# A fused retention and MLP kernel: chunk 0 of q and v loaded by SyncE as float32, a second bank for the first transposes, and four split units of the first product

## The chip, the cores and the metric

The kernel runs on one core of one Trainium2 chip. The metric is the time of one execution on the device in microseconds (us), lower is better; a kernel's time is the median of its runs. The five engines are PE (TensorE), DVE (VectorE), ACT (ScalarE), POOL (GpSimd) and SP (SyncE). Each takes its own instructions strictly in the order written, and they meet at semaphores.

## The reference

```python
def _attn_ref(q, k, v):                       # each (8, 8, 576, 64) float32
    scores = np.matmul(q, k.transpose(0, 1, 3, 2)) / np.sqrt(D_)
    gamma = 1.0 - 2.0 ** (-5.0 - np.arange(H))
    rel = pos[:, None] - pos[None, :]
    Dmat = np.where(rel >= 0, gamma[:, None, None] ** rel[None, :, :], 0.0)
    return np.matmul(scores * Dmat[None], v)
...
x = attn_out.transpose(0, 2, 1, 3).reshape(B * S, H * D)      # (4608, 512)
h = x @ w_in                                                  # (512, 2048)
g = h * (1.0 / (1.0 + np.exp(-1.702 * h)))
out = g @ w_out                                               # (2048, 512)
```

Attention without a softmax: each score is multiplied by gamma(head) to the power of the distance, and by zero for later keys. The two matrix products after it are most of the arithmetic.

## The kernel before, in words

**Recording.** The kernel is written as a list. `R.op(engine, function, reads, writes, banks)` (class `Rec`, line 43) appends one operation to its engine's queue and works out its waits from the named tiles and PSUM banks. So the order in which the Python calls stand is the order in which each engine works; there is no planner. An engine whose next operation waits does nothing else meanwhile.

**Attention of batch 0** works in chunks of 128 tokens: chunks 0 to 3 first, chunk 4 (64 tokens) later. For a chunk `n`:

- `load(0, n, "qkv")` (line 206) has POOL issue one DMA each for q, k and v, which turns float32 in DRAM into bfloat16 in `st_q`, `st_k`, `st_v`.
- `transposes(n)` (369) turns q and k on PE into the PSUM bank W (`psT`); `evac_t(n)` (378) copies the bank to `qk` on ACT.
- `intra(n)` (498) is `scores(n)` on PE into bank S, then `mask_s(n)` on DVE, which multiplies the scores by the mask into `sm`. For chunk 3 the mask is `mask3`, which has the decay factor in it, and `values(3)` takes v unscaled for the scores' part and the scaled copy `v3` for the state.
- `scale_v(n)` (352) multiplies v by the decay `vfac`: chunk 0 on DVE, chunks 1, 2 and 3 on POOL.
- `values(n)` (405) is three groups of eight matmuls on PE: scores times v, the running state k times v in bank Z, and q times the state so far (`zq`). With `z_last` the state comes last.
- `evac_z(n)` (465) copies the state on ACT; `evac_o(n)` (475) multiplies the result by `gq` on DVE and writes x transposed, `xT`, for the chunk's 128 tokens.

`later_gq` and `constants_first` make the decay tables with Exp on ACT; `fill(count)` (804) are matmuls of zeros that only keep PE running.

**The first product** of the 512 tokens of chunks 0 to 3 consists of 16 units f = 0 to 15 (`hidden`, 689): four matmuls of 512 columns with the weights `w_in`, then Gelu on ACT into `gT`. Unit f needs the weights' piece f // 2. The weights come in pieces `load_w_in(lo, hi)` (236): (0,1) for f = 0, 1; (1,2) for f = 2, 3; (2,4) for f = 4 to 7; (4,6); (6,8). Units 0 and 1 are made by `hidden_split` (704): first the columns of chunks 0 to 2 (0:384), then the columns of chunk 3 (384:512). The second product with `w_out` (`project`, 743) and the attention of batches 1 to 7 (`burst`) follow, unit by unit, with PE as the bound.

**The order around the change** is lines 786 to 876. POOL's queue: two iotas, the loads q0, k0, q1, k1, q2, k2, v0, q3, k3, v1, v2, v3, the weights (0,1), (1,2), (2,4), three `scale_v`, the other weights. PE's: 14 fills, turn 0, 4 fills, scores 0, turn 1, 3 fills, scores 1, turn 2, 3 fills, scores 2, turn 3, values 0, 3 fills, scores 3, values 1, 2 and 3, units 0 to 15. DVE's, after the constants: mask 0, mask 1, scale v0, mask 2, out 0, mask 3, out 1, out 2, out 3 ("mask n" is `mask_s(n)`, "out n" is `evac_o(n)`); then until about 35 us the memsets `constants_third`, `constants_shifted` and the swaps of `regroup`.

Of the kernel before, what the change touches and what calls it, by code (L numbers as in the profile page):

```python
# [131 lines left out]
def bass_retnet_parallel__then__act_gelu_quick_kernel(  # L132
# [11 lines left out]
    with es:  # L144
        def sb(name, shape, dtype):
            return es.enter_context(nc.sbuf_tensor(name, shape, dtype))
# [11 lines left out]
        tiny = sb("tiny", [P, 1], FP32)  # L158
        idle = sb("idle", [P, 512], BF16)
        lng = sb("lng", [P, HP], FP32)  # L160
        vraw = sb("vraw", [P, H, NC], FP32)
        vfac = [sb(f"vfac{i}", [P, H, NC], FP32) for i in range(2)]
        zacc = sb("zacc", [P, 3, 2 * 128], FP32)
# [30 lines left out]
        def gamma(h):  # L194
            return 1.0 - 2.0 ** (-5.0 - h)
# [40 lines left out]
        def load_w_in(lo, hi):  # L236

            cols = slice(256 * lo, 256 * hi)
            s = moe_w_in.rearrange("(a p) n -> p a n", p=128)[:, :, cols]
            R.op("POOL", lambda e: e.dma_start(w_in_sb[:, :, cols], s),  # L240
                 w=[("w_in", i) for i in range(lo, hi)], dma=("w_in", lo))
# [7 lines left out]
        def iota(t, name, pattern, base, mul):  # L249
            R.op("POOL", lambda e: e.iota(t.ap(), pattern, base=base, channel_multiplier=mul,  # L250
                                          allow_small_or_imprecise_dtypes=True), w=[name])

        def constants_first():
            iota(posj, "posj", [[128, NC]], 0, 1)
            iota(posa, "posa", [[1, 128]], 0, 0)
            R.op("DVE", lambda e: e.tensor_scalar(
                rel.ap(), posa.ap(), posj[:, 0:1], None, ALU.subtract),
                r=["posa", "posj"], w=["rel"])
            R.op("DVE", lambda e: e.memset(idle.ap(), 0.0), w=["idle"])
            for hp in range(HP):  # L260
                for hh in range(2):
                    R.op("DVE", lambda e, hp=hp, hh=hh: e.memset(
                        lng[64 * hh : 64 * hh + 64, hp : hp + 1],
                        math.log(gamma(2 * hp + hh))), w=[("lng", hp, hh)])
            R.op("DVE", lambda e: e.tensor_single_scalar(ident.ap(), rel.ap(), 0.0, ALU.is_equal),
                 r=["rel"], w=["ident"])
            R.op("DVE", lambda e: e.tensor_single_scalar(mask.ap(), rel.ap(), 0.0, ALU.is_ge),
                 r=["rel"], w=["mask"])
            for c in range(1, NC):
                R.op("DVE", lambda e, c=c: e.tensor_single_scalar(  # L270
                    posi[:, c - 1, :], posa.ap(), 128.0 * c, ALU.add), r=["posa"], w=["posi"])
            for h in range(H):
                R.op("ACT", lambda e, h=h: e.activation(
                    vraw[:, h, :], posj.ap(), AF.Exp, scale=-math.log(gamma(h))),
                    r=["posj"], w=["vraw"])
            for hp in range(HP):
                R.op("ACT", lambda e, hp=hp: e.activation(
                    gq[:, hp, 0:128], posa.ap(), AF.Exp, scale=lng[:, hp : hp + 1]),
                    r=["posa", ("lng", hp, 0), ("lng", hp, 1)], w=[("gq", 0)])
            R.op("DVE", lambda e: e.tensor_single_scalar(  # L280
                vfac[0].ap(), vraw.ap(), float(QK_SCALE), ALU.mult), r=["vraw"], w=[("vfac", 0)])

        def constants_second():
            R.op("DVE", lambda e: e.memset(zs.ap(), 0.0), w=[("zs", 0), ("zs", 1)])
# [67 lines left out]
        def scale_v(n, eng="DVE", to=None):  # L352
            b, c = divmod(n, NC)
            sl = b % NST
            t = st_v[:, sl, c, :].rearrange("p (h d) -> p h d", d=DH)
            f = vfac[min(b, 1)][:, :, c : c + 1].to_broadcast([P, H, DH])
            if to is None:
                R.op(eng, lambda e: e.tensor_tensor(t, t, f, ALU.mult),  # L358
                     r=[("vfac", min(b, 1))], w=[("v", sl, c)])
                return  # L360
            o = to.rearrange("p (h d) -> p h d", d=DH)
            R.op(eng, lambda e: e.tensor_tensor(o, t, f, ALU.mult),
                 r=[("vfac", min(b, 1)), ("v", sl, c)], w=[v3_key])

        def sides(n):
            b, c = divmod(n, NC)
            return [(0, st_q, "q", b % NST, c), (1, st_k, "k", b % NST, c)]

        def transposes(n):
            def fn(e):  # L370
                for a, t, nm, sl, c in sides(n):
                    for hp in range(HP):
                        i = e.matmul(psT[:, a, hp, :], t[:, sl, c, 128 * hp : 128 * hp + 128],  # L373
                                     ident.ap(), is_transpose=True)
                return i
            R.op("PE", fn, r=["ident"] + [(nm, sl, c) for a, t, nm, sl, c in sides(n)], ps=["W"])

        def evac_t(n):
            R.op("ACT", lambda e: e.activation(qk[n % NQK].ap(), psT, AF.Copy),  # L379
                 w=[("qk", n % NQK, 0), ("qk", n % NQK, 1)], ps=["W"])  # L380

        def half(r):
            return slice(64 * r, 64 * r + 64)
# [114 lines left out]
        def intra(n):  # L498
            scores(n)
            mask_s(n)  # L500
# [183 lines left out]
                R.op("DVE", lambda e: e.tensor_copy(z, zacc[:, 0 : len(gs), :]), r=r, w=["zw"])  # L684


        hbanks = [(psH[0], ("H", 0)), (psH[1], ("H", 1)), (psU, "U")]

        def hidden(c, f, at, ahead=()):
            bank, key = at  # L690
            toks = range(8 * c, 8 * c + 8)
# [1 line left out]
            def fn(e):  # L693
                for a in range(4):
# [9 lines left out]
        def hidden_split(fs):  # L704

            for lo, hi in ((0, 384), (384, 512)):
                for f in fs:
                    bank, key = hbanks[2 * f]

                    def fn(e, f=f, bank=bank, lo=lo, hi=hi):  # L710
                        for a in range(4):
                            i = e.matmul(bank[:, lo:hi], w_in_sb[:, a, 128 * f : 128 * f + 128],
                                         xT[:, a, lo:hi], start=(a == 0), stop=(a == 3))
                        return i
                    R.op("PE", fn, r=[("w_in", f // 2)]
                         + [("xT", x) for x in range(lo // 64, hi // 64)], ps=[key])
            for f in fs:
                bank, key = hbanks[2 * f]
                R.op("ACT", lambda e, f=f, bank=bank: e.activation(  # L719
                    gT[0][:, f, :], bank.ap(), AF.Gelu_apprx_sigmoid), w=[("gT", 0, f)], ps=[key])  # L720

        def hidden_half(c, half, f, at, ahead=()):
            bank, key = at
# [80 lines left out]
        def fill(count):  # L804
            def fn(e):
                for _ in range(count):
                    i = e.matmul(psH[0].ap(), idle[:, 0:128], idle.ap(), start=True, stop=True)
                return i
            R.op("PE", fn, r=["idle"], ps=[("H", 0)])
# [5 lines left out]
        fill(14)  # L815
# [36 lines left out]
        constants_third(0, NST)  # L852
        constants_shifted()
# [11 lines left out]
        turns = [0]  # L865
# [171 lines left out]
```

## Time and profile before

| | |
|---|---|
| median of 3 runs (lowest, highest) | 301.7 us (301.42, 302.22) |
| the profiled execution's own time | 302.22 us |
| its span, from first to last instruction | 300.4 us |
| busy share of the span: PE, DVE, ACT, POOL | 97%, 41%, 43%, 52% |
| granted TensorE clock | 0.999 |

The profiled execution is the slowest of the three; 1.8 us of its time lie outside the span. Times on the timeline are microseconds from the span's start. A line of the timeline gives the start, the duration, engine, source line, operation, the tile written and the tiles read, the shapes and the count, and in brackets how long the engine was idle before and who released it. Durations of consecutive operations on one engine overlap a little: the multiply by the mask lasts 1.23 us, but the next operation starts 1.14 us after it, and the 0.68 us of an `evac_o` are 0.60 to 0.62 us from start to start.

### The profile page before, as it was taken

How to read it: one execution, taken by the hardware profiler on the slowest of the kernel's cores; microseconds unless marked ns; L12 is line 12 of the kernel's file. 1: busy time of each engine (PE TensorE's matmuls, PEld its weight loads, DVE VectorE, ACT ScalarE, POOL GpSimd, SP SyncE). 2: the span in 40 equal slices, each digit the busy share in tenths (PEclk: the TensorE clock that was granted, in tenths of full speed). 3: DMA queues.
4: the chain of work that ended last, by engine and by line, in shares of the span. 5: the costliest groups of instructions: out<-in, count | busy, mean ns of one | idle time of the engine just before them, and what ended most of it. 6: DMA issues, size and time to landing. Idle time of an engine off the chain costs nothing.

```text
span 300.4 us, 7696 instructions
## 1 busy us (share of the span) xinstructions
PE 292.5 (97%) x3395; PEld 148.9 (50%) x3395; DVE 122.3 (41%) x213; ACT 127.9 (43%) x215; POOL 154.8 (52%) x208
## 2 busy tenths in 40 slices
PE   7899999899999999999999999999999999999996
PEld 3454455757645444444444444544444444444444
DVE  6589735362525555334506143265236503000012
ACT  7676426614445503560375036602570266026600
POOL 8999679998967868677985796000000000000000
PEclk9999999999999999999999999999999999999999
DMA  9999999999999999999999999904720210020012
GB/s 69 145 183 207 177 171 161 193 129 138 178 143 163 163 117 191 173 136 142 135 213 138 127 186 155 85 1 101 173 41 2 105 37 2 0 107 35 0 57 85
DMA packets 154850, 35.78 MB, mean 119 GB/s; under 512 B 145472, under 2 KB 150336, under 8 KB 154816
## 3 DMA queue, kind: packets, MB, share of 16 engines
q0 software_dynamic: 118384, 18.36, 95.8%
q1 hardware_dynamic: 36432, 16.92, 31.6%
q8 instruction: 27, 0.44, 0.6%
q14 instruction: 7, 0.06, 0.1%
HBM read 36.70 MB, written 9.44 MB: 154 GB/s over the span
## 4 chain that ended last, share of the span: by engine, by line
PE 88%; POOL 4%; DMA 3%; ACT 2%; DVE 1%; issue 1%; POOLq 0%
PE psH L746 27%; PE psH L695 24%; PE psU L746 13%; PE psU L695 12%; DMA w_in_sb<-in_moe_w_in_dram 3%; PE psA L560 2%; PE psA L588 2%; PE psH L730 2%; PE psA L602 1%; PE psA L576 1%; POOL st_q L216 1%; PE psA L746 1%; POOL st_k L216 1%; PE psA L772 1%; POOL st_v L216 1%; ACT qk L379 1%
## 5 line engine op out<-in xcount | busy, mean ns | idle before, releaser
L746 PE MATMUL psH<-w_out_sb,gT 128*128 128x512 bf16 x368 | 87.0, 379 | 0.0
L695 PE MATMUL psH<-xT,w_in_sb 128*128 128x512 bf16 x332 | 79.2, 379 | 0.2 <-DMA w_in_sb<-in_moe_w_in_dram 0.2
L649 DVE TENSOR_TENSOR xT<-psA,gq 128x768 bf16<-128x768 f32 x21 | 20.1, 958 | 115.2 <-PE psA L576 115.2
L700 ACT ACTIVATE gT<-psH 128x512 bf16<-128x512 f32 x83 | 49.5, 597 | 26.0 <-PE psH L695 26.0
L229 POOL DMA_DIRECT2D st_k<-in_k_dram x70 | 53.0, 782 | 14.1 <-DMA st_k<-in_k_dram 13.1
L746 PEld LDWEIGHTS psH<-w_out_sb,gT 128*128 128x128 bf16 x368 | 35.0, 98 | 40.7 <-DVE sm L660 0.4
L229 POOL DMA_DIRECT2D st_v<-in_v_dram x70 | 52.0, 770 | 6.0 <-DMA st_v<-in_v_dram 4.0
L695 PEld LDWEIGHTS psH<-xT,w_in_sb 128*128 128x128 bf16 x332 | 32.1, 98 | 38.6 <-DMA w_in_sb<-in_moe_w_in_dram 0.7
L695 PE MATMUL psU<-xT,w_in_sb 128*128 128x512 bf16 x172 | 44.2, 379 | 0.1
L746 PE MATMUL psU<-w_out_sb,gT 128*128 128x512 bf16 x176 | 43.9, 379 | 0.0
L216 POOL DMA_DIRECT2D st_q<-in_q_dram x40 | 36.0, 899 | 9.7 <-DMA st_q<-in_q_dram 7.3
L755 ACT ACTIVATE osb<-psH 128x512 f32<-128x512 f32 x21 | 12.5, 597 | 57.6 <-PE psH L746 54.5
L700 ACT ACTIVATE gT<-psU 128x512 bf16<-128x512 f32 x43 | 25.7, 597 | 13.5 <-PE psU L695 13.5
L695 PEld LDWEIGHTS psU<-xT,w_in_sb 128*128 128x128 bf16 x172 | 16.5, 98 | 20.0 <-ACT gT L719 0.6
L746 PEld LDWEIGHTS psU<-w_out_sb,gT 128*128 128x128 bf16 x176 | 16.6, 98 | 19.4 <-issue 0.5
L358 DVE TENSOR_TENSOR st_v<-st_v,vfac 128x512 bf16<-128x512 bf16 x37 | 24.2, 683 | 0.9 <-DMA st_v<-in_v_dram 0.9
L676 DVE TENSOR_TENSOR zacc<-zacc,psA 128x256 f32<-128x256 f32 x49 | 20.5, 418 | 8.3 <-PE psA L588 7.1
L755 ACT ACTIVATE osb<-psU 128x512 f32<-128x512 f32 x10 | 6.0, 597 | 33.0 <-PE psU L746 33.0
L660 DVE TENSOR_TENSOR sm<-psA,maskw 128x768 bf16<-128x768 f32 x21 | 19.9, 948 | 0.0
L379 ACT ACTIVATE qk<-psA 128x1024 bf16<-128x1024 bf16 x10 | 10.2, 1022 | 10.5 <-PE psA L373 10.5
L758 DVE COPY osb<-psH 128x512 f32<-128x512 f32 x2 | 1.4, 692 | 26.9 <-PE psH L746 26.9
L560 PEld LDWEIGHTS psA<-sm,st_v 64*64 64x64 bf16 x504 | 7.5, 108 | 9.4 <-issue 8.7
(103 smaller groups left out, 231.0 us busy)
## 6 DMA issues: line engine op xcount, KB each, us to landing
out_dram<-osb SPq DMA_DIRECT2D x35, 256.0 KB, 4.0
st_q<-in_q_dram POOLq DMA_DIRECT2D x32, 128.0 KB, 7.2
st_k<-in_k_dram POOLq DMA_DIRECT2D x57, 64.0 KB, 7.5
st_v<-in_v_dram POOLq DMA_DIRECT2D x57, 64.0 KB, 7.3
w_out_sb<-in_moe_w_out_dram POOLq DMA_DIRECT2D x4, 512.0 KB, 11.8
w_in_sb<-in_moe_w_in_dram POOLq DMA_DIRECT2D x3, 512.0 KB, 8.9
st_k<-in_k_dram POOLq DMA_DIRECT2D x4, 128.0 KB, 4.5
st_v<-in_v_dram POOLq DMA_DIRECT2D x4, 128.0 KB, 4.6
```

The costliest lines, as they stand in the source:

```text
L216: paced(R.op("POOL", lambda e, d=d, s=s: e.dma_start(d, s), w=[(nm, sl, c)], dma=(nm, sl, c), own=pace()))
L229: paced(R.op("POOL", lambda e: [e.dma_start(d, s) for d, s in parts], w=[(nm, sl, c)], dma=(nm, sl, c), parts=2, own=pace()))
L358: R.op(eng, lambda e: e.tensor_tensor(t, t, f, ALU.mult), r=[("vfac", min(b, 1))], w=[("v", sl, c)])
L379: R.op("ACT", lambda e: e.activation(qk[n % NQK].ap(), psT, AF.Copy), w=[("qk", n % NQK, 0), ("qk", n % NQK, 1)], ps=["W"])
L560: i = e.matmul(psA[half(t), 2 + u, at : at + 64], rows_of(st_v, m_out, g, u, 4 * u + 2 * t + j), smw[si(m_out)][half(r), j, 2 * blk + t, : ...
L649: R.op("DVE", lambda e: e.tensor_tensor(xT[:, :, t0 : t0 + 192].rearrange("p (u j) n -> p u j n", u=2), psA[:, 2:4, 0:384].rearrange("p u ...
L660: R.op("DVE", lambda e: e.tensor_tensor(o, i, k, ALU.mult), r=["maskw"], w=[("sm", si(m))], ps=["S"])
L676: R.op("DVE", lambda e, to=to, src=src, was=was: e.tensor_tensor(to, was, src, ALU.add), r=[("zacc", (blk - 1) % 3)], w=[("zacc", blk)], p ...
L695: i = e.matmul(bank, w_in_sb[:, a, 128 * f : 128 * f + 128], xT[:, a, 512 * c : 512 * c + 512], start=(a == 0), stop=(a == 3))
L700: R.op("ACT", lambda e: e.activation(gT[c % 2][:, f, :], bank, AF.Gelu_apprx_sigmoid), w=[("gT", c % 2, f)], ps=[key])
L746: i = e.matmul(bank, gT[c % 2][:, f, 128 * r : 128 * r + 128], w_out_sb[:, f, :], start=(f == 0), stop=(f == NF - 1))
L755: R.op("ACT", lambda e: e.activation(osb[m].ap(), bank, AF.Copy), w=[("osb", m)], ps=[key])
```

## The change

- **Loads.** q and v of chunk 0 are no longer loaded by POOL with a cast. SP issues them as float32 into two pieces of `gT[1]` that are unused then (`early(0)`, `early(1)`). DVE casts q0 into `st_q`; `scale_v(0)` reads the float32 v0 and writes `st_v`, and stands right after the constants instead of after turn 2.
- **POOL's queue** becomes: k0, two iotas, q1, k1, v1, q2, k2, v2, q3, `scale_v(1)`, k3, w_in (0,1) and (1,2), v3, w_in (2,4), `scale_v(3)`, w_in (4,6) and (6,8), w_out. `scale_v(2)` moves from POOL to DVE, between out 1 and out 2.
- **Banks.** The transposes of chunks 1 and 3 go to bank H0 (`psH[0]`) instead of W; the fills go to H1.
- **Constants.** The zeros for the fills and the logarithms come before anything that waits for POOL; eight Exp become one; `mask` and three of four `posi` come after `scale_v(0)`.
- **PE's order:** 13 fills, turn 0, 3 fills, turn 1, scores 0, 2 fills, turn 2, scores 1, values 0, 2 fills, scores 2, values 1, 3 fills, turn 3, values 2, scores 3, units 0 and 1 on columns 0:384, values 3, units 2 and 3 on columns 0:384, units 0 to 3 on columns 384:512, then units 4 to 15 whole. Unit 4 goes to bank S.
- **DVE's order** from mask 0 on: mask 0, mask 1, out 0, mask 2, out 1, scale v2, out 2, the memset `zs`, mask 3, out 3.

```diff
+        def load_early(i, src):
+            s = src[0, :, 0:128, :].rearrange("h p d -> p h d")
+            d = early(i).rearrange("p (h d) -> p h d", d=DH)
+            R.op("SP", lambda e: e.dma_start(d, s), w=early_keys(i), dma=("early", i))
...
+            R.op("ACT", lambda e: e.activation(vraw.ap(), vraw.ap(), AF.Exp, scale=-1.0), w=["vraw"])
...
+            R.op("DVE", lambda e: e.tensor_copy(st_q[:, 0, 0, :], early(0)),
+                 r=early_keys(0), w=[("q", 0, 0)])
             R.op("DVE", lambda e: e.tensor_single_scalar(
                 vfac[0].ap(), vraw.ap(), float(QK_SCALE), ALU.mult), r=["vraw"], w=[("vfac", 0)])
+            scale_v(0)
+            for c in range(2, NC):
+                position(c)
+            R.op("DVE", lambda e: e.tensor_single_scalar(mask.ap(), rel.ap(), 0.0, ALU.is_ge),
+                 r=["rel"], w=["mask"])
...
+            if n == 0:
+                i = early(1).rearrange("p (h d) -> p h d", d=DH)
+                R.op(eng, lambda e: e.tensor_tensor(t, i, f, ALU.mult),
+                     r=[("vfac", 0)] + early_keys(1), w=[("v", sl, c)])
+                return
...
+        def turned(n):
+            if n < NC - 1 and n % 2:
+                return psH[0].ap().bitcast(BF16).rearrange("p (a h n) -> p a h n", a=2, h=HP), ("H", 0)
+            return psT, "W"
...
+        constants_zero()
+        load_early(0, q)
+        load_early(1, v)
+        load(0, 0, "k")
         constants_first()
-        for c in range(3):
-            load(0, c, "qk")
-        load(0, 0, "v")
-        load(0, 3, "qk")
-        for c in range(1, 4):
-            load(0, c, "v")
+        load(0, 1, "qk")
+        load(0, 1, "v")
+        load(0, 2, "qk")
+        load(0, 2, "v")
+        load(0, 3, "q")
+        scale_v(1, "POOL")
+        load(0, 3, "k")
         load_w_in(0, 1)
         load_w_in(1, 2)
+        load(0, 3, "v")
         load_w_in(2, 4)
-        scale_v(1, "POOL")
-        scale_v(2, "POOL")
         scale_v(3, "POOL", v3)
...
+        split = [(psW, "W"), (psU.ap(), "U"), (psH[1].ap(), ("H", 1)), (psH[0].ap(), ("H", 0))]
+
+        def hidden_part(f, lo, hi):
+            bank, key = split[f]
+
+            def fn(e):
+                for a in range(4):
+                    i = e.matmul(bank[:, lo:hi], w_in_sb[:, a, 128 * f : 128 * f + 128],
+                                 xT[:, a, lo:hi], start=(a == 0), stop=(a == 3))
+                return i
+            R.op("PE", fn, r=[("w_in", f // 2)] + [("xT", x) for x in range(lo // 64, hi // 64)],
+                 ps=[key])
+            if hi == 512:
+                R.op("ACT", lambda e: e.activation(gT[0][:, f, :], bank, AF.Gelu_apprx_sigmoid),
+                     w=[("gT", 0, f)], ps=[key])
+
+        fill(13)
         transposes(0)
+        evac_t(0)
         later_gq(0)
-        later_gq(1)
-        evac_t(0)
-        constants_second()
         constants_mask3()
-        later_gq(2)
-        fill(4)
-        intra(0)
+        fill(3)
         transposes(1)
         evac_t(1)
-        later_gq(3)
-        fill(3)
-        intra(1)
+        intra(0)
+        later_gq(1)
+        fill(2)
         transposes(2)
         evac_t(2)
-        scale_v(0)
-        fill(3)
+        intra(1)
+        values(0, third[0])
+        evac_z(0)
+        evac_o(0, third[0])
+        later_gq(2)
+        later_gq(3)
+        fill(2)
         intra(2)
-        transposes(3)
-        evac_t(3)
-        values(0, third[0])
-        evac_o(0, third[0])
-        evac_z(0)
-        fill(3)
-        intra(3)
         values(1, third[1])
         evac_z(1)
         evac_o(1, third[1])
+        scale_v(2)
+        fill(3)
+        transposes(3)
+        evac_t(3)
         values(2, third[0])
         evac_z(2)
         evac_o(2, third[0])
+        constants_second()
         gelu_table()
-        values(3, third[2], z_last=True)
-        evac_o(3, third[2])
+        intra(3)
+        hidden_part(0, 0, 384)
+        hidden_part(1, 0, 384)
+        values(3, third[0], z_last=True)
+        evac_o(3, third[0])
+        hidden_part(2, 0, 384)
+        hidden_part(3, 0, 384)
+        for f in range(4):
+            hidden_part(f, 384, 512)
         evac_z(3)
...
         regroup("gq")
-        hidden_split(range(2))
-        for f in range(2, NF):
+        regroup(0)
+        hidden(0, 4, (psA[:, 0, :], "S"))
+        for f in range(5, NF):
             hidden(0, f, next_bank())
```

More of the change, by code (lines that the diff above doesn't have):

```diff
@@ L160, in bass_retnet_parallel__then__act_gelu_quick_kernel @@
         lng = sb("lng", [P, HP], FP32)
+        lnh = sb("lnh", [P, H], FP32)
         vraw = sb("vraw", [P, H, NC], FP32)
@@ L251, in iota, with early, early_keys, constants_zero @@
                                           allow_small_or_imprecise_dtypes=True), w=[name])
+        def early(i):
+            return gT[1][:, 2 * i : 2 * i + 2, :].rearrange("p f n -> p (f n)").bitcast(FP32)
+        def early_keys(i):
+            return [("gT", 1, 2 * i), ("gT", 1, 2 * i + 1)]
+        def load_early(i, src):
+            s = src[0, :, 0:128, :].rearrange("h p d -> p h d")
+            d = early(i).rearrange("p (h d) -> p h d", d=DH)
+            R.op("SP", lambda e: e.dma_start(d, s), w=early_keys(i), dma=("early", i))
+        def constants_zero():
+            R.op("DVE", lambda e: e.memset(idle.ap(), 0.0), w=["idle"])
+            for h in range(H):
+                R.op("DVE", lambda e, h=h: e.memset(lnh[:, h : h + 1], math.log(gamma(h))),
+                     w=["lnh"])
+            for hh in range(2):
+                R.op("DVE", lambda e, hh=hh: e.tensor_copy(
+                    lng[64 * hh : 64 * hh + 64, :], lnh[64 * hh : 64 * hh + 64, hh : H : 2]),
+                    r=["lnh"], w=[("lng", hp, hh) for hp in range(HP)])
         def constants_first():
@@ L255, in constants_first @@
             iota(posa, "posa", [[1, 128]], 0, 0)
+            R.op("DVE", lambda e: e.tensor_tensor(
+                vraw.ap(), posj.ap().unsqueeze(1).to_broadcast([P, H, NC]),
+                lnh.ap().unsqueeze(2).to_broadcast([P, H, NC]), ALU.mult),
+                r=["posj", "lnh"], w=["vraw"])
             R.op("DVE", lambda e: e.tensor_scalar(
@@ L258, in constants_first, with position @@
                 r=["posa", "posj"], w=["rel"])
[L259 to L264, printed above, removed]
             R.op("DVE", lambda e: e.tensor_single_scalar(ident.ap(), rel.ap(), 0.0, ALU.is_equal),
                  r=["rel"], w=["ident"])
[L267 to L270, printed above, removed]
+            def position(c):
+                R.op("DVE", lambda e: e.tensor_single_scalar(
                     posi[:, c - 1, :], posa.ap(), 128.0 * c, ALU.add), r=["posa"], w=["posi"])
[L272 to L275, printed above, removed]
+            position(1)
+            R.op("ACT", lambda e: e.activation(vraw.ap(), vraw.ap(), AF.Exp, scale=-1.0), w=["vraw"])
             for hp in range(HP):
@@ L367, in sides @@
             return [(0, st_q, "q", b % NST, c), (1, st_k, "k", b % NST, c)]
+        def turned(n):
+            if n < NC - 1 and n % 2:
+                return psH[0].ap().bitcast(BF16).rearrange("p (a h n) -> p a h n", a=2, h=HP), ("H", 0)
+            return psT, "W"
         def transposes(n):
+            to, key = turned(n)
             def fn(e):
@@ L372, in fn @@
                     for hp in range(HP):
-                        i = e.matmul(psT[:, a, hp, :], t[:, sl, c, 128 * hp : 128 * hp + 128],
+                        i = e.matmul(to[:, a, hp, :], t[:, sl, c, 128 * hp : 128 * hp + 128],
                                      ident.ap(), is_transpose=True)
                 return i
-            R.op("PE", fn, r=["ident"] + [(nm, sl, c) for a, t, nm, sl, c in sides(n)], ps=["W"])
+            R.op("PE", fn, r=["ident"] + [(nm, sl, c) for a, t, nm, sl, c in sides(n)], ps=[key])
         def evac_t(n):
-            R.op("ACT", lambda e: e.activation(qk[n % NQK].ap(), psT, AF.Copy),
-                 w=[("qk", n % NQK, 0), ("qk", n % NQK, 1)], ps=["W"])
+            to, key = turned(n)
+            R.op("ACT", lambda e: e.activation(qk[n % NQK].ap(), to, AF.Copy),
+                 w=[("qk", n % NQK, 0), ("qk", n % NQK, 1)], ps=[key])
         def half(r):
@@ L684, in state_wide @@
                 R.op("DVE", lambda e: e.tensor_copy(z, zacc[:, 0 : len(gs), :]), r=r, w=["zw"])
-        hbanks = [(psH[0], ("H", 0)), (psH[1], ("H", 1)), (psU, "U")]
         def hidden(c, f, at, ahead=()):
@@ L702, in hidden @@
                  w=[("gT", c % 2, f)], ps=[key])
[L704 to L720, printed above, removed]
         def hidden_half(c, half, f, at, ahead=()):
@@ L806, in fn @@
                 for _ in range(count):
-                    i = e.matmul(psH[0].ap(), idle[:, 0:128], idle.ap(), start=True, stop=True)
+                    i = e.matmul(psH[1].ap(), idle[:, 0:128], idle.ap(), start=True, stop=True)
                 return i
-            R.op("PE", fn, r=["idle"], ps=[("H", 0)])
+            R.op("PE", fn, r=["idle"], ps=[("H", 1)])
         def quarters(bank):
@@ L814, in bass_retnet_parallel__then__act_gelu_quick_kernel @@
         third = [(psO, "O"), (quarters(psU), "U"), (quarters(psH[1]), ("H", 1))]
-        fill(14)
+        split = [(psW, "W"), (psU.ap(), "U"), (psH[1].ap(), ("H", 1)), (psH[0].ap(), ("H", 0))]
[12 more added lines that the diff above has]
+        fill(13)
         transposes(0)
+        evac_t(0)
         later_gq(0)
-        later_gq(1)
-        evac_t(0)
-        constants_second()
         constants_mask3()
-        later_gq(2)
-        fill(4)
-        intra(0)
+        fill(3)
         transposes(1)
         evac_t(1)
-        later_gq(3)
-        fill(3)
-        intra(1)
+        intra(0)
+        later_gq(1)
+        fill(2)
         transposes(2)
         evac_t(2)
-        scale_v(0)
-        fill(3)
-        intra(2)
-        transposes(3)
-        evac_t(3)
-        values(0, third[0])
-        evac_o(0, third[0])
-        evac_z(0)
-        fill(3)
-        intra(3)
+        intra(1)
[5 more added lines that the diff above has]
+        fill(2)
+        intra(2)
         values(1, third[1])
@@ L863, in bass_retnet_parallel__then__act_gelu_quick_kernel @@
                       (psA[:, 2, :], "O")]
-        turns = [0]
+        turns = [1]
         def next_bank():
```

## The prediction

> **What bounds the kernel now.** I read the page's chain of work first, then the chain of the first 60 us in order of time. The shares say PE:
>
> ```profile
> PE 88%; POOL 4%; DMA 3%; ACT 2%; DVE 1%; issue 1%; POOLq 0%
> ```
>
> The chain in order of time says where the other shares lie. All of them up to 22.4 us are one string:
>
> ```profile
> 9.42 2.62 POOL st_v L216 x3
> 12.04 1.37 POOL w_in_sb L240 x2
> 13.41 8.94 DMA w_in_sb<-in_moe_w_in_dram
> 22.35 0.05 issue
> 22.39 1.90 PE psH L695 x8
> ```
>
> Twelve loads go out on POOL one after the other, then the weight pieces; piece (2,4) leaves at 13.41 and lands at 22.35, and unit 4 starts at 22.39. From there PE works without a pause: the remaining twelve units take 22.39 to 32.93, 0.88 each. So the change is worth what it moves **the start of unit 4**, if nothing behind it gives it back.
>
> The timeline shows how PE came there. Units 0 and 1 start at 18.24, their columns 384:512 at 19.55, unit 2 at 20.00. Without the wait for weights unit 4 would start two whole units later, at about 20.00 + 2 x 0.87 = 21.7. The DMA is thus only 0.7 us ahead of a second limit, the attention of chunks 0 to 3, which runs on DVE:
>
> ```profile
> 11.43 1.23 DVE L402 TENSOR_TENSOR sm<-psA,mask 128x1024 bf16<-128x1024 f32 x1 [0.93 <-PE psA L392]
> 12.57 0.68 DVE L358 TENSOR_TENSOR st_v<-st_v,vfac 128x512 bf16<-128x512 bf16 x1
> 13.59 1.22 DVE L402 TENSOR_TENSOR sm<-psA,mask 128x1024 bf16<-128x1024 f32 x1 [0.34 <-PE psA L392]
> 14.73 0.68 DVE L480 TENSOR_TENSOR xT<-psA,gq 128x512 bf16<-128x512 f32 x1
> 15.75 1.23 DVE L402 TENSOR_TENSOR sm<-psA,gT 128x1024 bf16<-128x1024 f32 x1 [0.34 <-PE psA L392]
> 16.89 0.68 DVE L480 TENSOR_TENSOR xT<-psU,gq 128x512 bf16<-128x512 f32 x1
> 17.49 0.68 DVE L480 TENSOR_TENSOR xT<-psA,gq 128x512 bf16<-128x512 f32 x1
> 18.11 0.69 DVE L480 TENSOR_TENSOR xT<-psH,gq 128x512 bf16<-128x512 f32 x1
> ```
>
> These are masks 1, 2 and 3, scale v0 and the four outs: almost no gaps. A shorter load phase helps only as far as this string moves too.
>
> **The change, part by part.**
>
> *The loads.* POOL's rows:
>
> ```profile
> 1.37 1.04 POOL L216 DMA_DIRECT2D st_q<-in_q_dram  x1 [0.20 <-issue]
> 2.41 0.90 POOL L216 DMA_DIRECT2D st_k<-in_k_dram  x1
> ...
> 5.88 0.92 POOL L216 DMA_DIRECT2D st_k<-in_k_dram  x1
> ```
>
> The first costs 1.04, each later one 0.87 from start to start. Asked for the narrow windows around these issues, the DMA view gives 3.7 us to landing for the first, 4.3 and 4.4 for the next, 4.5 for k2 (so it lands at 10.4), 4.7 for k3. After the change k0 leaves at about 0.8, the iotas take 0.33 and the restart 0.20, so q1 leaves at 2.4, k1 at 3.2, v1 at 4.1, q2 at 5.0 and **k2 at 5.84: the sixth load, as before**, since v1 has moved ahead of it where q0 moved away. It lands at 10.35. Two loads fewer gain chunk 2 nothing.
>
> *Turn 0 and turn 1.* k0 lands near 0.8 + 3.7 = 4.5 (6.7 before), and the 13 fills then set turn 0: the zeros are ready at about 1.0, a fill takes 0.43 (the spacing of its weight loads), so turn 0 comes at 6.1 to 6.6 instead of 7.1. Turn 1 waits for k1 (7.6), mask 0 ends by about 10.1. All of this ends before k2 lands: nothing gained, nothing lost. The second bank only frees turn 1 from the copy of turn 0, which is not on the path either. One Exp of eight (0.24 each) is hidden in the same way.
>
> *The SP loads.* No row shows a load on SP. The nearest rows are its stores (0.33 to 1.44 us of issue, 2.0 to 7.9 to landing) and its DMA transposes, which move pieces of 256 bytes too (1.2 to 2.4, then 2.4 to 9.4). v0 as the second thus lands between 0.75 + 0.33 + 2.0 = 3.1 and 0.75 + 2.4 + 9.4 = 12.5. The upper end comes from times with ten microseconds of DMA queued; at 1 us nothing is queued, and the row of the same shape is POOL's own first load, 3.7. I take q0 at 4.5, v0 at 5.7. SP is free: its first other work is at 48. Behind v0 on DVE stand scale v0 0.68, three `posi` at 0.39 (the mean in the groups by form), `mask` 0.66, two products for `mask3` 1.42 and mask 0 1.23, together 5.2; mask 1 can start at 11.4, so the cover holds **until v0 lands at 6.2**, and each microsecond beyond costs one.
>
> *The string on DVE.* Turn 2 starts 0.15 after k2 (as turn 0 did: 6.75, 6.90) at 10.5, takes 0.41 of weight loads, scores 1 follow, and the mask comes 0.47 after them (10.96, 11.43): mask 1 at M = 11.4, by chance as before. From M: out 0 at M + 1.14; scores 2 get bank S 0.1 after mask 1 ends, so mask 2 at 1.23 + 0.1 + 0.47 = M + 1.80; out 1 at + 2.94; scale v2, new here, at + 3.54, done at + 4.22. `values(2)` must wait for it: 0.91 on PE (16.47 to 17.38) and 0.09 of handing over, so out 2 at + 5.22. Then the memset `zs` (0.31) at + 5.83, mask 3 at + 6.14, done at + 7.37. Before, the outs filled the time in which PE worked; now PE's 0.91 stands in the string.
>
> *PE's end.* While mask 3 runs, PE does units 0 and 1 on 384 columns (1.31, from 18.24 to 19.55) between out 2 and the end of mask 3: + 5.9 to + 7.2, just hidden. `values(3)` starts at + 7.42 and takes 0.93 to the next product (17.31 to 18.24): + 8.35. Units 2 and 3 on 384 columns: 1.31. Four pieces of 128 columns: 2 x 0.45 (19.55 to 20.00 is two). Sum: **unit 4 at M + 10.56 = 22.0**. This is the gain from splitting: behind `values(3)` stand 2.2 us of PE instead of the 3.5 of four whole units, but `values(3)` starts 1.5 us later (18.8 against 17.3).
>
> *POOL as a worker.* `scale_v(1)` now stands before k3. v1 lands at 4.1 + 4.4 = 8.5, just when q3's issue ends; with 1.17 us and 0.2 of restart k3 leaves at 9.9 (8.47 before), (0,1) at 10.8, (1,2) at 11.5, v3 at 12.3 (11.1 before). k3 lands at 13.6 to 14.4 by 3.7 or 4.5; turn 3, at 14.7 behind three fills, does not feel it. v3 lies behind two weight pieces: before, v3 landed at 16.0 and they at 17.8 and 19.8, 1.9 each, so v3 lands at 14.4 + 3.8 + 0.9 = 19.1 at the latest; at the earliest, with the two pieces' 512 KB at the 207 GB/s of the page's fourth slice (2.5 us) behind a k3 at 13.6, at 17.0. The landing gaps are the nearer row, but with a queue that POOL's own multiply has let run empty: I take 18.4. Then `scale_v(3)`, 1.17, and the state of `values(3)` may start at 19.65, where the string on DVE would let it at 11.4 + 8.1 = 19.5. So **unit 4 at 22.1**. Piece (2,4) leaves at 13.1 and lands at about 21; (4,6) waits behind `scale_v(3)`, leaves at 19.7 and lands by 25, where unit 8 needs it at 25.6.
>
> *Behind it.* Unit 4 in bank S never waits for a Gelu. Out 3 ends at M + 8.9 = 20.3 instead of 18.8, so DVE's 16 us of memsets and swaps end 1.5 later; the wait behind them is 1.96 long (the mask at 37.09, released by PE) and shrinks by PE's 0.3 too, so the cover holds by 0.1 to 0.2, with 1.1 more until PE's `values` at 38.9 feel it.
>
> Sum: 22.39 to 22.1, **0.3 us less**. The profiled execution would go from 302.22 to 301.9 (span 300.1); it was the slowest of three, so against the median of 301.7 I predict **301.4**.
>
> **Rivals.**
>
> 1. *The loads come sooner, faster.* If an emptier queue brings all loads after 3.7 instead of 4.5, k2 lands at 9.55, M is 10.6 and unit 4 at 21.2, v3 allowing (it must land by 17.4): 1.2 less, 300.5. For it: 3.7 was measured. Against: the queue in front of k2 is as long as before. 0.18.
> 2. *v3 through POOL, slower.* One mechanism: k3, two weight pieces, v3, `scale_v(3)` in one order, and PE's state waits for the last. It decides from v3 landing at 18.3 on; at 18.7 all is lost, and each later microsecond costs one. If v1 lands 0.6 late beside SP's loads, POOL starts everything behind it 0.6 late, and by the later bound v3 lands at 19.7: unit 4 at 23.4, 1.0 more, 302.7. For it: the landing gaps of 1.9 behind a full queue. 0.17.
> 3. *SP's loads hold up POOL's.* If their two chunks pass the DMA engines first, at the 0.87 that each load takes, k2 lands 1.74 late, M is 13.1 and unit 4 at 23.7: 1.3 more, 303.0. Against: the view by stretches shows nothing moving before 3 us and 98 GB/s from 3 to 6 against 151 from 6 to 9, so there is room. v0 past 6.2 works the same way. 0.08.
>    The Trainium skill, "DMA: Bandwidth & Descriptors", section "Issuing engines are not separate DMA queues", says that DMAs issued by any engine run on the same 16 DMA engines and that several issuers save only issue time; this speaks for rival 3 and against any gain in landing.
>    The same page, section "Latency and other measured facts", gives a first byte after about 0.6 us for SP against 1 us for POOL, which no run here shows yet; by it v0 lands inside its cover and the sum stays.
> 4. *The gain is there and DVE's later string takes it back*, the mask of chunk 4 coming late: no change, 301.7. 0.10.
>
> **How the numbers follow.** Forecast 0.47. Faster or slower by over 0.3% is 0.9 us, about what a measurement of this kernel tells from no change. Rival 1 is the faster case: 0.18. Rivals 2 and 3 are the slower ones: 0.25. Forecast and rival 4 lie within: 0.57. The range leaves out a tenth on each side: beyond rival 1's 300.5 by 0.3, and reaches past rival 2's 302.7 by 0.2: 300.2 to 302.9.
>
> **What would show it.** Right: mask 1 within 0.3 of 11.4; a wait of DVE before mask 3 or out 2 for `values(2)`; unit 4 at 22.1, with no wait for piece (2,4). Rival 1: mask 1 before 11. Rival 2: a PE wait at line 427 for `gT` from POOL. Rival 3: k2 landing past 11. Rival 4: a PE wait near 37 to 39. Wrong altogether: a PE clock below 1 after the new gaps in front of turn 2, or a wait after 40 us that is new.

## The result and the profile after

The changed kernel takes 304.69 us (median of 4 runs, 303.91 to 305.63) against 301.96 for the kernel before beside it: ratio 1.0081, 95% interval 1.0054 to 1.0108. Run again later, it gave 303.84 against 302.12, ratio 1.0058 (1.0036 to 1.0080). It is **slower by 1.75 and 2.45 us** by these two ratios, where 0.3 less was forecast. The profiled execution took 303.91, its span is 302.0. The ratios leave out executions more than 1.5% longer than the fastest of their kernel and the medians don't, which shows in one place, experiment e12.

The page's chain by engine, where DMA had 3%:

```profile
PE 81%; DMA 9%; POOL 4%; ACT 2%; issue 2%; DVE 1%; POOLq 0%; ACTq 0%
```

The chain of the first 60 us in order of time (start, us, what):

```profile
12.71 6.71 DMA st_v<-in_v_dram
19.43 0.07 issue
19.50 1.05 POOL gT L391
20.55 1.51 POOL w_in_sb L241 x2
22.06 1.48 POOL w_out_sb L246 x2
23.55 0.64 POOL st_q L217
24.18 12.04 DMA st_k<-in_k_dram
36.22 0.14 issue
36.36 0.61 PE psA L409 x8
...
49.27 0.02 issue
49.29 0.61 ACT osb L772
49.90 0.02 issue
49.91 3.46 DMA out_dram<-osb
```

Before, the string of loads ended in the weights for unit 4. Now it runs on past the first product: v3 lands at 19.43, POOL multiplies it, and only then issues the remaining weights and chunk 4's loads; k4 (`st_k` of chunk 4) lands at 36.22, and turn 4 on PE waits for it. Further on in this profile, ACT waits for a store; the chain of the second profile has no such step.

The rows on DVE and POOL that answer to those of before:

```profile
12.05 1.23 DVE L439 TENSOR_TENSOR sm<-psA,mask 128x1024 bf16<-128x1024 f32 x1 [1.48 <-PE psA L429]
...
17.18 0.69 DVE L517 TENSOR_TENSOR xT<-psA,gq 128x512 bf16<-128x512 f32 x1 [0.98 <-PE psA L479]
...
18.06 1.16 DVE L439 TENSOR_TENSOR sm<-psA,gT 128x1024 bf16<-128x1024 f32 x1
...
19.50 1.05 POOL L391 TENSOR_TENSOR gT<-st_v,vfac 128x512 bf16<-128x512 bf16 x1 [5.11 <-DMA st_v<-in_v_dram]
...
20.36 0.69 DVE L517 TENSOR_TENSOR xT<-psA,gq 128x512 bf16<-128x512 f32 x1 [1.14 <-PE psA L479]
```

POOL stands still for 5.11 us in front of its multiply. In numbers, before to after:

| | before | after | after, again |
|---|---|---|---|
| mask 1 starts | 11.43 | 12.05 | 11.78 |
| v3 lands | 15.97 | 19.43 | 18.52 |
| unit 4's weight load | 22.39 | 23.00 | 22.15 |
| k4 lands | 33.84 | 36.22 | 35.68 |
| turn 4's first matmul | 34.49 | 36.36 | 35.81 |
| first copy into `osb` | 47.42 | 49.29 | 48.75 |
| last copy into `osb` | 297.86 | 299.42 | 299.21 |

(Landing times are an issue's start plus the DMA view's time to landing.) In the second profile unit 4 is 0.24 *earlier* than before, and the kernel is still 1.35 later at the end. So unit 4, on which the prediction rested everything, is not where the time went; turn 4 is: from unit 4 to turn 4 before takes 12.1, after 13.4 and 13.7. Turn 4's first transposes on PE, before and then after:

```profile
34.49 0.39 PE L373 MATMUL psA<-ident,st_q 128*128 128x128 bf16 x4
...
36.36 0.38 PE L409 MATMUL psA<-ident,st_q 128*128 128x128 bf16 x4 [1.05 <-DMA st_k<-in_k_dram]
```

Before, PE came to them straight from the matmul in front; after, it stood 1.05 us until k4 had landed.

### The profile page after: what moved, and what is told of

The parts are those of the page before. It is cut to its first block, busy times and chain, and to the rows that moved or that the text cites. A ratio compares the mean times of both kernels' runs of the same rounds, so it can differ in the third digit from the quotient of the medians.

```text
span 302.0 us, 7662 instructions
## 1 busy us (share of the span) xinstructions
PE 286.6 (95%) x3364; PEld 148.8 (49%) x3399; DVE 124.7 (41%) x218; ACT 125.8 (42%) x208; POOL 152.2 (50%) x205
## 4 chain that ended last, share of the span: by engine, by line
PE 81%; DMA 9%; POOL 4%; ACT 2%; issue 2%; DVE 1%; POOLq 0%; ACTq 0%
PE psH L763 25%; PE psH L730 21%; PE psU L763 12%; PE psU L730 11%; DMA st_k<-in_k_dram 4%; DMA st_v<-in_v_dram 4%; PE psA L597 2%; PE psA L625 2%; PE psH L747 2%; PE psA L639 1%; PE psA L613 1%; PE psA L789 1%; DMA out_dram<-osb 1%; ACT qk L416 1%; POOL w_in_sb L241 1%
## 5 line engine op out<-in xcount | busy, mean ns | idle before, releaser
L763 PE MATMUL psH<-w_out_sb,gT 128*128 128x512 bf16 x352 | 83.8, 379 | 2.0 <-issue 1.7
L730 PE MATMUL psH<-xT,w_in_sb 128*128 128x512 bf16 x319 | 77.0, 379 | 1.0 <-issue 0.6
L735 ACT ACTIVATE gT<-psH 128x512 bf16<-128x512 f32 x82 | 48.7, 597 | 25.1 <-PE psH L730 25.1
L763 PE MATMUL psU<-w_out_sb,gT 128*128 128x512 bf16 x171 | 42.6, 379 | 0.8 <-issue 0.8
L730 PE MATMUL psU<-xT,w_in_sb 128*128 128x512 bf16 x162 | 41.7, 379 | 0.3 <-issue 0.3
L217 POOL DMA_DIRECT2D st_q<-in_q_dram x39 | 35.2, 903 | 9.3 <-DMA st_q<-in_q_dram 6.0
L735 ACT ACTIVATE gT<-psU 128x512 bf16<-128x512 f32 x41 | 24.5, 597 | 12.6 <-PE psU L730 12.6
L730 PEld LDWEIGHTS psU<-xT,w_in_sb 128*128 128x128 bf16 x164 | 15.8, 98 | 19.0 <-ACT gT L735 0.3
L416 ACT ACTIVATE qk<-psA 128x1024 bf16<-128x1024 bf16 x8 | 8.2, 1022 | 12.3 <-PE psA L409 12.3
```

Of the source, the lines that this page charges most:

```text
L217: paced(R.op("POOL", lambda e, d=d, s=s: e.dma_start(d, s), w=[(nm, sl, c)], dma=(nm, sl, c), own=pace()))
L416: R.op("ACT", lambda e: e.activation(qk[n % NQK].ap(), to, AF.Copy), w=[("qk", n % NQK, 0), ("qk", n % NQK, 1)], ps=[key])
L730: i = e.matmul(bank, w_in_sb[:, a, 128 * f : 128 * f + 128], xT[:, a, 512 * c : 512 * c + 512], start=(a == 0), stop=(a == 3))
L763: i = e.matmul(bank, gT[c % 2][:, f, 128 * r : 128 * r + 128], w_out_sb[:, f, :], start=(f == 0), stop=(f == NF - 1))
```

## The experiments

Theory: POOL's order is the cause. `scale_v(3)` waits for a v3 that was put behind two weight pieces, and everything issued behind it, k4 above all, comes late. Rivals: the longer string on DVE; SP's loads in the same DMA engines; the bank; PE's clock. All runs are compared with the kernel before on the same chip.

**e1, `scale_v(3)` behind the remaining weights.**

```diff
         load_w_in(2, 4)
-        scale_v(3, "POOL", v3)
         load_w_in(4, 6)
...
         load_w_out(1)
+        scale_v(3, "POOL", v3)
```

> The changed kernel with one edit: POOL multiplies v3 (scale_v(3)) behind the issues of the remaining weights instead of in front of them. Theory (POOL's order): POOL no longer sits idle for 5.1 us with issues behind it; the weights (4,6) to w_out land 2 us sooner, k4 lands by 34.5, PE's wait of 1.7 us in front of turn 4 goes, and unit 4 stays at 23.0 because v3 lands as late as now: 1.2 us less than the changed kernel, about 303.5. Rival (the string on DVE is all of it): nothing behind unit 4 matters, 304.7 as now. Rival (SP's loads): 304.7 as now.

302.88, ratio 1.0020 (1.0000 to 1.0040). POOL's row:

```profile
18.72 1.05 POOL L391 TENSOR_TENSOR gT<-st_v,vfac 128x512 bf16<-128x512 bf16 x1 [1.64 <-DMA st_v<-in_v_dram]
```

POOL now waits 1.64 with nothing urgent behind it, k4 lands at 33.34, turn 4 starts at 34.43, and the first copy into `osb` at 47.36, level with before. From unit 4 to turn 4 it is 12.1 us, as before the change. The interval of the time touches the second one of the unedited kernel (1.0036 to 1.0080), so it is these rows that carry the reading, and not the time alone. Unit 4 itself came at 22.29, not 23.0: v3 landed 0.8 sooner, as it did in the second profile of the unedited kernel, so that part is scatter of the load stream and not the edit. Turn 4 came at 35.81 in that second profile, though, so an early v3 alone does not bring it to 34.43.

**e2, v3 loaded in front of the weights.**

```diff
         load(0, 3, "k")
+        load(0, 3, "v")
         load_w_in(0, 1)
         load_w_in(1, 2)
-        load(0, 3, "v")
```

> The changed kernel with one edit: v3 is loaded right behind k3, in front of the weight pieces (0,1) and (1,2). Theory (POOL's order): v3 lands near 15 instead of 19.4, the values of chunk 3 wait for nothing, scale_v(3) is done by 16.5, POOL goes on 3 us sooner; unit 4 at 22.5 and no wait in front of turn 4: about 1.8 us less than the changed kernel, 302.8. Rival (the string on DVE): unit 4 comes no sooner than 22.9, at most 0.2 less, 304.5. Rival (SP's loads): as the string's.

302.01, ratio 0.9993 (0.9972 to 1.0013): all of the loss is gone. Unit 4 at 22.50, turn 4 at 34.64. The expectation of 302.8 was too careful. The changed rest of the kernel, with DVE's longer string, SP's loads and both banks, costs nothing that can be measured: the first three rivals fall as causes of the loss. The fourth, PE's clock, has no place in the profiles: the granted clock is 1.00 between 15 and 36 us in both of the changed kernel.

**e3, as e2, with the iotas first and `scale_v(1)` behind v3's load.**

```diff
+        iota(posj, ...); iota(posa, ...)
         load(0, 0, "k")
...
         load(0, 3, "q")
-        scale_v(1, "POOL")
         load(0, 3, "k")
         load(0, 3, "v")
+        scale_v(1, "POOL")
```

> As the kernel with v3 loaded behind k3, and two more edits in POOL's queue: the iotas before k0 as in the kernel before, and scale_v(1) behind the load of v3 instead of in front of k3's. Theory: the first load of POOL leaves at 1.37 either way, so q1 to k2 leave 0.25 sooner and mask 1 starts at 11.8 instead of 12.05; k3, v3 and the weights leave 1.4 sooner; unit 4 at 22.2, about 302.4, 0.3 to 0.4 less than with v3 alone. Rival (SP's loads hold up POOL's): mask 1 stays at 12.0 and nothing is gained over v3 alone.

302.51, ratio 1.0016 (0.9996 to 1.0036); not told apart from e2. k2 left at 5.97 instead of 6.16 in e2 but landed at 10.88 instead of 10.96, and mask 1 came at 12.00 instead of 12.08: here the rival was right.

**e4, only the SP loads, in the kernel before.** q0 and v0 by `load_early` as in the change, q0 cast on DVE, `scale_v(0)` at its old place, POOL's queue otherwise as before.

> The kernel before with one part of the change: q0 and v0 loaded by SP as float32 (cast of q0 on DVE behind posi, scale_v(0) reading float32 at its old place). Theory (the loads are not what costs): POOL's queue is two loads shorter, piece (2,4) leaves 1.7 sooner and lands by 21.3, so its wait of 0.7 in front of unit 4 goes and the attention sets unit 4 at 21.8: 0.5 less than before, 301.4. Rival (SP's loads hold up POOL's on the DMA engines): k1 to k3 land 0.5 to 1.7 later than in the kernel before, the same or up to 1 us more, 302 to 303.

302.39, ratio 1.0003 (0.9978 to 1.0028). The profile shows both at once. k2 leaves POOL at 5.03 instead of 5.88, yet lands at 10.23 instead of 10.40: the two loads moved to SP pass through the same stream. But piece (2,4) lands at 19.96 instead of 22.35, unit 4 starts at 21.42 instead of 22.39, and the first copy into `osb` comes 0.77 sooner. That gain is in the profile and not in the median; its executions lie between 300.9 and 304.0.

**e5, as e3, with q2 and k2 in front of v1.**

```diff
+        load(0, 2, "qk")
         load(0, 1, "v")
-        load(0, 2, "qk")
         load(0, 2, "v")
```

> The kernel with v3 first, iotas first and scale_v(1) late, and one more edit: POOL issues q2 and k2 in front of v1. In that kernel mask 1 starts at 12.0 because turn 2 waits for k2, which lands at 10.9. Theory (all loads share one stream of about 0.9 us per load, so the place in the stream decides): k2 is the seventh load of all instead of the eighth, lands at 10.0 to 10.2, mask 1 at 11.2 to 11.4, unit 4 at 21.7 instead of 22.4, about 0.7 less than that kernel: 301.8. Rival (the steps of PE, ACT and DVE set mask 1, which follows mask 0 by 2.15 in the kernel before): mask 1 no sooner than 11.4 whatever the loads do. Rival (SyncE's loads cost nothing): k2 lands 4.5 after its issue as in the kernel before, at 9.6.

301.86, ratio 0.9995 (0.9973 to 1.0017). In this profile v0 landed at 6.13 instead of 5.3 to 5.5, mask 0 started at 9.97 instead of 9.2, k2 landed at 10.35, mask 1 at 11.69: half of what was expected. Unit 4 came no sooner (22.55). Piece (0,1) landed late too, at 17.77, but unit 0's first weight load, at 18.06, waited 0.63 us for out 2 and not for the piece: out 2 started at 17.32 where e3 had 17.12, so the 0.3 us won at mask 1 were lost between mask 1 and out 2 (5.63 instead of 5.12). There the multiply of v2 on DVE, `scale_v(2)`, took 1.18 us from 15.16 on, where it took 0.68 in e3. For the first 0.6 of it POOL was at its own multiply of v3 (14.69 to 15.78); in e3 POOL's had just ended as DVE's began. That the two multiplies get in each other's way is likely from this, but no run here tests it.

**e6, as e3, with `scale_v(2)` right behind mask 1.**

```diff
         intra(1)
+        scale_v(2)
         values(0, third[0])
...
         evac_o(1, third[1])
-        scale_v(2)
```

> The kernel with v3 first, iotas first and scale_v(1) late, and one more edit: scale_v(2) stands on DVE right behind mask 1 instead of behind out 1. Theory (the string on DVE sets unit 4, and values(2) stand in it because they wait for v2): values(2) then wait only for mask 2, out 2 comes at about 16.6 instead of 17.1 and unit 4 0.5 sooner, 0.5 less than that kernel: 302.0. Rival (loads or weights set unit 4): no change, 302.5.

301.86, ratio 0.9989 (0.9971 to 1.0007). From mask 1 to out 2 it is 4.54 instead of 5.12, so the string is 0.58 shorter, as worked out; unit 4 at 21.98 instead of 22.36. The string on DVE is real, but it is not what the change lost.

**e7, both edits.**

> Both edits: q2 and k2 in front of v1, and scale_v(2) right behind mask 1. Theory: they add, unit 4 at 21.2, where the weights (2,4), landing at 21.1, take over as the bound: 1.1 to 1.2 less than the kernel with neither, 301.3, and about 1 us less than the kernel before. Rival (the weights bind sooner): no better than one of the two edits alone.

301.26, ratio 0.9971 (0.9954 to 0.9987): **0.9 us faster than the kernel before**, the only version whose interval lies wholly below it, though it overlaps that of e6. Mask 1 starts at 11.00. What binds then is not piece (2,4) but (0,1), which landed at 17.40 where e3 had 15.45 (PE's row in e7, unit 0's part on 384 columns):

```profile
17.54 0.81 PE L843 MATMUL psA<-xT,w_in_sb 128*128 128x384 bf16 x4 [1.33 <-DMA w_in_sb<-in_moe_w_in_dram]
```

So unit 4 came at 22.01, where 21.2 was expected and e6 had 21.98: the weights took back what mask 1 had won, as the rival said. The expected time was met by luck and not by the mechanism. Where the 0.9 us come from is not shown; a part is that this profile has no pause of PE near 65 us (the last section tells of it).

**e8, as e3, without the split.**

```diff
-        hidden_part(0, 0, 384)
-        hidden_part(1, 0, 384)
         values(3, third[0], z_last=True)
...
+        for f in range(4):
+            hidden(0, f, split[f])
```

> The kernel with v3 first, iotas first and scale_v(1) late, but units 0 to 3 of the first product whole and behind values(3), without the split at column 384. Theory (two pieces of 384 columns, 1.3 us, lie hidden beside mask 3): unit 4 comes 1.3 later, 303.8. Rival (the split gains nothing, because something else binds unit 4): the same, 302.5.

308.28, ratio 1.0200 (1.0173 to 1.0227): 5.8 more than e3, where 1.3 was expected. The view by stretches (PE, PEld, DVE, ACT, POOL busy, then the granted clock, DMA share, GB/s):

```profile
15.00:18.00 3.00, 1.94 (x42) 1.34 (x40) 2.02 (x4) 2.18 (x3) 3.00 (x5) 1.00 1.24 166
18.00:21.00 3.00, 1.56 (x24) 1.08 (x24) 1.70 (x3) 0.71 (x2) 0.38 (x1) 0.69 1.19 183
21.00:24.00 3.00, 2.34 (x6) 1.04 (x8) 2.50 (x6) 0.60 (x1) 1.38 (x2) 0.50 1.24 207
24.00:27.00 3.00, 3.00 (x11) 1.12 (x9) 2.78 (x10) 1.19 (x2) 2.66 (x4) 0.67 1.24 204
```

PE idles 1.81 us beside mask 3 (17.46 to 19.27), then the granted clock falls to 0.50 and comes back only near 26 (two thirds of full speed between 24 and 27). The pieces of 384 columns do not only hide 1.3 us, they keep PE at full clock.

**e10, as e8, with seven fills between scores 3 and values 3** (`fill(7)` behind `intra(3)`).

> The kernel without the split, with one edit: seven matmuls of zeros stand on PE between scores 3 and values 3, where the split pieces were. Theory (without the pieces PE idles for 2 us beside mask 3 and its clock is halved for some microseconds, and that was most of the 6 us lost): the clock stays at 1 and unit 4 comes about 1.5 later than with the split, 304.0. Rival (the lost microseconds are the lost overlap itself): 308 as without the fills.

306.04, ratio 1.0124 (1.0103 to 1.0146). The clock stays at 1.00 in every stretch; unit 4 at 24.30 against 26.82 without the fills and 22.36 with the split. So of 4.5 us at unit 4 the clock was 2.5 and the lost overlap 1.9, of which some 0.3 is a later mask 1 (12.28 against 12.00 in e3). The time expected, 304.0, was missed by 2: in this profile a pause of 1.15 at 67.5, told below, comes on top.

**e11, as e3, with the one bank W.**

> The kernel with v3 first, iotas first and scale_v(1) late, and all first transposes in the one bank W as before the change. Theory (the second bank is not on the path, turn 1 waits for k1): the same within 0.3, 302.5. Rival (the second bank carries a part of the result): turn 1 waits for the copy of turn 0, and units 0 on 384 columns for the copy of turn 3: up to 1 us more.

302.41, ratio 1.0018 (0.9999 to 1.0036), unit 4 at 22.25: the second bank is not on the path.

**e9, the changed kernel again**, unedited.

> The changed kernel once more, unedited: its first four times lie in two pairs, 303.9 and 304.1, 305.3 and 305.6, and the profile is of the shortest. Theory (POOL's order alone): the times stay between 303.5 and 306 with a mean 2 to 2.7 above before, and a longer execution would show a longer wait for k4 in front of turn 4. Rival (PE's clock): in the longer executions PE's gaps let the granted clock drop for some microseconds, as in the kernel without the split, and the profile of such a one shows a clock below 1 between 15 and 36 us.

The numbers stand above. Its profile is again of a short execution (303.6), with the clock at 1.00 between 15 and 36 us. The mean clock of each execution on record says more: it is 1.000 in those of 305.32 and 305.63 of the first measurement and in the one of 304.84 here, against 0.988 to 0.989 in those of e8, where the clock did fall; the only lowered one here, 0.994, belongs to the shortest, 302.83. So a fallen clock is not what a 305 holds. What it does hold stays open.

**e12, the other way round: v3 behind two weight pieces in the kernel before.**

```diff
-        for c in range(1, 4):
+        for c in range(1, 3):
             load(0, c, "v")
         load_w_in(0, 1)
         load_w_in(1, 2)
+        load(0, 3, "v")
```

> The kernel before with one edit of the change: v3 is loaded behind the weight pieces (0,1) and (1,2). Theory (this place in POOL's queue is what costs): v3 lands at 19.5 instead of 16.0, scale_v(3) starts then instead of at 16.2, (4,6) and all loads behind it leave 3 us later, the values of chunk 3 wait from 17.3 to 19.5 on PE, and unit 4 starts at 23.9 instead of 22.4; k4 lands near 36 instead of 33.8, hidden or not by PE's own delay: 1.5 to 2.2 more than before, 303.8 to 304.5. Rival (the order hurts only together with the longer string on DVE or with SP's loads): within 0.5 of before.

307.30 against 301.94, ratio 1.0129 (1.0073 to 1.0184). The order alone, with nothing else of the change, makes the kernel before slower, by its median at least as much as the change did (the intervals overlap). PE's rows:

```profile
19.22 0.41 PE L415 MATMUL psH<-sm,st_v 128*64 128x128 bf16 x8 [1.82 <-DMA st_v<-in_v_dram]
...
20.27 0.43 PE L427 MATMUL psA<-gT,st_k 128*64 128x64 bf16 x8 [0.29 <-POOL gT L362]
20.62 1.46 PE L712 MATMUL psH<-xT,w_in_sb 128*128 128x384 bf16 x4
```

`values(3)` waits 1.82 us for v3, and the four matmuls of 384 columns then take 1.46 instead of 0.82: PE's clock fell here too (0.61 between 21 and 24). Unit 4 starts at 25.48, expected 23.9; 0.29 of the rest is the wait for POOL, most of it the clock. This profile is of an execution of 309.2, with a mean clock of 0.989 (three of the others have 0.994 and one 0.983), so the clock's part differs from one to the next. Turn 4 comes at 37.78, 12.3 after unit 4 and straight behind the matmul in front, with no wait for k4. So e12 shows what v3's place costs in front of unit 4; the path through k4 is shown by e1 and not by this run.

## Why the prediction was wrong

**What bounds the kernel** was read rightly, and so was most of the path to unit 4. Forecast 22.1, measured 23.00 and 22.15. Term by term:

- *The loads.* k0 was to leave POOL at 0.8. It left at 1.25 after a wait on POOL's own queue, so that putting it in front of the iotas gained 0.1 (1.37 before) and held the iotas up by 1.5. k2 then left at 6.14 instead of 5.84 and needed 4.8 to land instead of 4.5: mask 1 came at 12.05, forecast 11.4. In the second profile k2 left at 6.14 too and landed 4.5 later, as forecast, with mask 1 at 11.78. So rival 3, SP's chunks in POOL's stream, is at most 0.3 in one profile of two, a sixth of its price; in e4 k2 needs 5.20 to land instead of 4.52. What the Trainium skill says in "DMA: Bandwidth & Descriptors", section "Issuing engines are not separate DMA queues", is borne out by e4: another issuer saved 0.85 at the issue of k2 and 0.17 at its landing.
- *The SP loads* landed at 4.1 and 5.4, forecast 4.5 and 5.7. The cover held.
- *The string on DVE* from mask 1: out 2 at + 5.13, mask 3 at + 6.01, out 3 at + 8.31 (+ 8.08 in the second profile), forecast 5.22, 6.14 and about 8.2. Right.
- *v3 through POOL*: forecast 18.4, landed at 19.43 and 18.52. In the first profile this cost the string 0.2 and the state 0.3.

**The step that failed is "Behind it".** The part on POOL followed piece (4,6) to unit 8, found it in time, and stopped there; the part behind unit 4 looked at DVE alone. The loads of chunk 4 stand at the end of the same queue, behind `scale_v(3)`. With POOL still for 5.1 us, the DMA stream ran thin (the stretch from 21 to 24 us after, then in e3; the last three figures are the clock, the DMA share and GB/s):

```profile
21.00:24.00 3.00, 2.95 (x28) 2.05 (x28) 2.50 (x6) 1.42 (x3) 3.00 (x5) 1.00 0.54 79
...
21.00:24.00 3.00, 3.00 (x29) 1.87 (x26) 2.67 (x7) 2.06 (x5) 1.80 (x3) 1.00 1.24 206
```

(1.03 and 140 in the second profile.) k4 landed 2.4 late, while PE needs it two units into the second product. Before, k4 landed at 33.84 and PE needed it at 34.49: a margin of 0.65 that no sentence of the prediction names, though its own times for POOL put piece (4,6) at 19.7 where it had left at 17.20, 2.5 later, with k4 still behind it. At the first copy into `osb` the first profile is 1.9 late, 0.6 from unit 4 and 1.3 from turn 4; the second is 1.3 late, 1.6 from turn 4 less 0.2 at unit 4. e1 shows it by moving the one line, which brings turn 4 to 34.43; e2 by taking the wait away, which takes all of the loss.

**Rival 2** had the right place and the slower sign, and was mispriced: it counted v3's lateness once, through PE's state, and said that all is lost from v3 at 18.7 on. With v3 at 18.52, unit 4 was on time and 1.3 us were lost all the same. Its sign, a wait of PE for `gT` from POOL, did appear in the first profile, at 0.29 us, and not in the second. Rival 4 did not happen: PE's wait near 36 was for k4, not for chunk 4's mask. The gain itself, 0.3, was of a size that no run here could have shown.

**Open:** the two profiles end 1.35 and 1.6 us later than that of before; the ratios say 1.75 and 2.45. No profile of an execution of 305 was taken; by the clock on record (e9) it is not PE's clock.

## What to carry to other kernels

A multiply that has to wait for its input, put into an engine's queue of DMA issues, delays every load issued behind it, also those needed much later: follow the queue to its end and write the margin of each transfer beside it, not only of the one next on the path. Order a shared stream of loads by when each is needed, and put a computation that waits behind all issues that don't depend on it. Where PE must wait beside another engine, give it work: what it loses there can be its clock as well.

## What the runs showed of the hardware

- PE's granted clock fell to 0.5 after an idle time of 1.81 us (e8) and after one of 1.82 (e12), both with several shorter gaps ahead of them, and was back at 1.00 only 3 to 7 us later (0.50 from 20 to 25 us and 1.00 from 26 in e8; 0.50 from 20 to 23 and 1.00 from 24 in e12). In e10, with seven matmuls in the gap, it stayed at 1.00. In the changed kernel, with two pieces of work in the same place, it stayed at 1.00. The Trainium skill, "TensorE: Matmul & The Clock Gate", Part 1, names half rate as the cold state, which agrees, and gives windows of about 3.4 us of idling for it; here 1.8 us with sparse work ahead were enough.
- In an early step of the other batches' attention PE pauses in the middle of a group of matmuls, near 65 us (up to 70 in the later kernels), with nothing to wait for ("issue"): 0.24 in the profile before and in e5, 0.40 in e3, 0.49 in e4, 1.15 in e10 and e11, 1.20 in e6, 1.31 in e8, 2.04 in e12, none in both of the changed kernel, e1, e2 and e7. It is always at the same place of PE's program, and in all nine profiles that have it, it ends 2.5 to 3.1 us after the start of a packet of 16 KB of the DMA queue named for instructions. In the nine, PE came to that place 1.0 to 2.6 us after the packet, in the five without a pause 2.7 to 3.8 us after it. That fits a PE waiting for its own instructions, but no run tests it. Whatever its cause, it shifts what follows it in one profile against another by up to 2 us.
- POOL's first DMA left at 1.25 when it stood first in the queue and at 1.37 behind two iotas.
- A multiply of 128 x 512 on DVE took 1.18 us in e5, the first 0.6 of it beside a multiply on POOL, and 0.68 in e3, just after POOL's had ended.
